# Fused attention and gMLP on one core: f32 loads cast on chip, half-size products paired in column halves, and a gMLP that runs without its lag

## The chip, the cores and the metric

The kernel runs on one core of one Trainium2 chip. The metric is device time in microseconds (us), the median of several runs. Engines are named as in the profile: PE is TensorE (matrix products), PEld its weight loads, DVE VectorE, ACT ScalarE, POOL GpSimd, SP SyncE (which here only issues transfers). In the traces below each engine takes its own instructions in the order of the program (VectorE's turns at 98.82 us, for example, behind five normalizations that they don't need), and the engines meet one another through semaphores. SBUF is the memory in which the kernel's tiles lie, PSUM the one in which this program puts PE's products. "Granted clock" is the share of full speed that PE was allowed.

## The reference, cut to what matters

There are 8 batches of 8 heads, 576 tokens, 64 numbers per head. Attention is causal with a window of 64 tokens; its result, 576 x 512 per batch, goes into a gated MLP that mixes over tokens.

```python
scores = scale * q @ k.T ; keep only 0 <= row - col < 64 ; attn = softmax(scores) @ v
x = attn.transpose(0, 2, 1, 3).reshape(8, 576, 512)
h = relu(x @ w_in)                         # w_in 512 x 1024
u, v = h[..., :512], h[..., 512:]
v_n = (v - mean(v)) / sqrt(var(v) + 1e-6)  # over the 512 features
v_s = w_spatial @ v_n + b_spatial          # over the 576 tokens
out = (u * v_s) @ w_out                    # w_out 512 x 512
```

## The kernel before

All inputs are f32 in DRAM; the products run in f16. The parts of the work have one-letter names that the whole text uses. For attention: T turns Q and K (VectorE transposes), S is the scores of two heads, E their exponential and mask, P the product with V and with ones. N1 and N2 are the logarithm and the exponential that turn P's row sums into reciprocals, and the multiplication that gives x. For the gMLP: V and U are the two halves of x @ w_in, L the normalization of V, G the product with w_spatial and the gate, O the product with w_out. W is the transposition of w_spatial, once.

V is needed at two alignments of 64 tokens, hence a copy shifted by 64 tokens ("vs" beside "vn").

```python
def load_qk(b, x, g, hp):                      # the load casts f32 to f16 on its way
    s = SRC[x][b, 4 * hp + g, :, :].rearrange("(k i t) d -> i k (t d)", i=32, t=2)
    nc.gpsimd.dma_start(NAT[b, x][32 * g:32 * g + 32, hp, :, :, :]..., s)

def emit_O(b, j):                              # 5 of them per batch, the fifth for 64 tokens
    po = mm(f"po{b}_{j}")
    for r in range(4):
        nc.tensor.matmul(po[0:jn, :], lhs, w_out_sb[r][:, :], start=(r == 0), stop=(r == 3))
    nc.scalar.copy(ob[0:jn, :], po[0:jn, :])
    (nc.scalar if b < 2 else nc.sync).dma_start(out[...], ob[0:jn, :])

def att_step(i, s, todo, before, between):     # one of the five steps of attention
    run_units(todo, before)                    # gMLP work first ...
    emit_S(i, s) ; post += [emit_E]
    emit_P(pb, ps_) ; post += [emit_N1, emit_N2]   # P of the step before
    while post:
        post.pop(0)()
        run_units(todo, between)               # ... and gMLP work between

for i in range(2, B + 2):                      # the steady state
    a, o = i - 1, i - 2                        # attention of i, gMLP of i-1, O of i-2
    st[0] = O(o);  st[1] = V(a);  st[2] = L(a), U0, U1, U2;  st[3] = G0, U3, G1, U4;  st[4] = G2, G3, G4
    # Q and K of batch i+1 are turned one piece per step, behind the steps 1 to 4 of batch i
    ...
```

So three batches are in work at a time: O lags the rest of its gMLP by one batch, and the turns of a batch stand in the steps of the batch before it. (The loop is shortened here.)

The softmax here doesn't subtract the row's maximum and nothing guards it: scores larger than these inputs give would overflow.

## Time and profile before

The kernel took 261.0 us at first; beside the changed kernel it took 262.45 us (median of 4 runs, 259.44 to 263.96). The profiled run has a span of 262.4 us.

| stage, by the start of V's first product of a batch | before, us |
|---|---|
| first scores | 20.2 |
| V of batch 0 | 36.2 |
| V of batch 1 | 84.5 |
| from V of batch 1 to V of batch 7, six periods | 155.2 |
| last three periods | 24.2, 24.2, 23.6 |
| the rest after V of batch 7 starts | 22.7 |

The page's busy line and its 40 slices, before. A digit is the busy share of a slice in tenths (a slice is 6.6 us), PEclk is the granted clock and DMA the mean busy share of the 16 DMA engines.

```profile
PE 218.9 (83%) x2899; PEld 111.8 (43%) x2899; DVE 154.8 (59%) x301; ACT 152.0 (58%) x283; POOL 151.5 (58%) x234
PE   8009884973965987998998699999999999999993
PEclk9756998696895799999999989999999999999999
DMA  8992499999999942995969995499330032004005
```

PE has holes in its first 23 slices, to about 151 us, and is full after that. There are two regimes, then: start-up and data at first, PE later. The DMA queues, before (packets, MB, share of 16 engines' span):

```profile
q0 software_dynamic: 46016, 12.27, 48.2%
q1 hardware_dynamic: 36816, 15.34, 25.6%
```

The view of windows for two late periods, before. Columns: window, its length, then busy time (and number) of PE, PEld, DVE, ACT, POOL, the granted clock, the DMA share and GB/s.

```profile
164.00:188.20 24.20, 23.89 (x359) 12.51 (x362) 17.70 (x35) 17.68 (x34) 17.60 (x27) 1.00 0.93 148
188.20:212.40 24.20, 24.10 (x359) 12.43 (x362) 17.72 (x35) 18.05 (x34) 5.82 (x7) 1.00 0.15 51
```

PE is busy 23.9 and 24.1 of 24.2 us: a late period is PE's work and almost nothing else. The view of waits, before: who waited for what, total us, times, longest us. These are PE's two largest.

```profile
PE sc L209 <- DVE tq L79: 14.2, 2, 13.6
PE oz L272 <- DVE x L300: 11.1, 12, 2.2
```

The first, all but 0.6 us of it, is the start (the first scores). No wait for x is longer than 2.2 us.

### The profile page before, as it was taken

How to read it: one execution, taken by the hardware profiler on the slowest of the kernel's cores; microseconds unless marked ns; L12 is line 12 of the kernel's file. 1: busy time of each engine (PE TensorE's matmuls, PEld its weight loads, DVE VectorE, ACT ScalarE, POOL GpSimd, SP SyncE). 2: the span in 40 equal slices, each digit the busy share in tenths (PEclk: the TensorE clock that was granted, in tenths of full speed). 3: DMA queues.
4: the chain of work that ended last, by engine and by line, in shares of the span. 5: the costliest groups of instructions: out<-in, count | busy, mean ns of one | idle time of the engine just before them, and what ended most of it. 6: DMA issues, size and time to landing. Idle time of an engine off the chain costs nothing.

```text
span 262.4 us, 6988 instructions
## 1 busy us (share of the span) xinstructions
PE 218.9 (83%) x2899; PEld 111.8 (43%) x2899; DVE 154.8 (59%) x301; ACT 152.0 (58%) x283; POOL 151.5 (58%) x234
## 2 busy tenths in 40 slices
PE   8009884973965987998998699999999999999993
PEld 2004541441534434544554345545544554554351
DVE  0076644353347598739770968397759757771740
ACT  2004962651276574576763685778687587856523
POOL 8631886599999979999863975985660000000000
PEclk9756998696895799999999989999999999999999
DMA  8992499999999942995969995499330032004005
GB/s 131 185 187 39 61 169 208 132 131 184 111 238 201 140 43 24 142 202 52 128 69 185 190 140 58 162 194 174 84 116 1 2 121 66 0 2 165 17 0 180
DMA packets 84175, 30.41 MB, mean 116 GB/s; under 512 B 77424, under 2 KB 79536, under 8 KB 84144
## 3 DMA queue, kind: packets, MB, share of 16 engines
q0 software_dynamic: 46016, 12.27, 48.2%
q1 hardware_dynamic: 36816, 15.34, 25.6%
q10 hardware_dynamic: 1312, 2.36, 2.7%
q8 instruction: 22, 0.36, 0.6%
q14 instruction: 9, 0.07, 0.1%
HBM read 32.79 MB, written 9.44 MB: 161 GB/s over the span
## 4 chain that ended last, share of the span: by engine, by line
PE 37%; DMA 17%; DVE 14%; POOL 14%; ACT 13%; issue 4%; ACTq 0%; DVEq 0%; POOLq 0%
PE ps L373 10%; PE po L394 8%; DMA out_dram<-ob 6%; DVE st L326 5%; PE pv L321 5%; DMA nq<-in_q_dram 5%; POOL nq L68 4%; POOL vs L122 3%; PE sc L209 3%; DVE x L300 3%; DMA nk<-in_k_dram 3%; PE oz L272 3%; POOL nk L68 3%; DMA wnat<-in_moe_w_spatial_dram 3%; ACT vs L324 2%
## 5 line engine op out<-in xcount | busy, mean ns | idle before, releaser
L122 POOL COPY vs<-vn 64x1024 f16<-64x1024 f16 (+1 forms) x44 | 42.5, 965 | 17.9 <-ACT vn L128 10.2
L249 ACT ACTIVATE e<-sc 128x1024 f16<-128x1024 f32 x32 | 32.7, 1021 | 21.5 <-PE sc L209 19.8
L68 POOL DMA_DIRECT2D nq<-in_q_dram x64 | 38.4, 616 | 10.0 <-issue 3.1
L373 PE MATMUL ps<-wspT,vn 128*128 128x512 f16 (+1 forms) x160 | 41.6, 393 | 2.8 <-DVE vn L343 2.6
L300 DVE TENSOR_TENSOR x<-oz,zi 128x512 f16<-128x512 f32 (+1 forms) x40 | 25.4, 634 | 30.3 <-ACT zi L298 26.4
L68 POOL DMA_DIRECT2D nk<-in_k_dram x64 | 38.6, 614 | 4.1 <-DMA wnat<-in_moe_w_spatial_dram 1.3
L321 PE MATMUL pv<-win,x 128*128 128x512 f16 (+1 forms) x160 | 39.6, 394 | 0.0
L394 PE MATMUL po<-wout,g 128*128 128x512 f16 (+1 forms) x160 | 38.0, 380 | 0.0
L209 PE MATMUL sc<-tq,tk 32*64 32x128 f16 (+2 forms) x1152 | 24.9, 222 | 15.1 <-DVE tq L79 14.2
L326 DVE BATCH_NORM_STATS2 st<-vs 128x6 f32<-128x512 f16 (+1 forms) x40 | 27.3, 683 | 14.4 <-ACT vs L324 14.1
L258 DVE TENSOR_TENSOR e<-e,mask 128x1024 f16<-128x1024 f16 x32 | 26.3, 822 | 15.4 <-ACT e L249 15.1
L397 ACT COPY ob<-po 128x512 f32<-128x512 f32 (+1 forms) x40 | 23.3, 583 | 20.7 <-PE po L394 12.8
L209 PEld LDWEIGHTS <-tk 32*64 32x64 f16 x1280 | 20.8, 109 | 32.1 <-issue 16.8
L353 PE MATMUL pu<-x,win 128*128 128x512 f16 x128 | 34.0, 406 | 0.0
L290 ACT ACTIVATE ln<-oz 128x512 f32<-128x512 f32 (+1 forms) x40 | 22.4, 560 | 10.4 <-PE oz L282 9.5
L324 ACT ACTIVATE vs<-pv 128x512 f16<-128x512 f32 (+1 forms) x40 | 23.5, 597 | 8.1 <-PE pv L321 7.3
L376 DVE TENSOR_TENSOR g<-ps,ru 128x512 f16<-128x512 f32 x32 | 21.1, 674 | 10.4 <-PE ps L373 10.2
L298 ACT ACTIVATE zi<-ln 128x512 f32<-128x512 f32 (+1 forms) x40 | 23.7, 592 | 1.3 <-ACT ob L397 0.8
L373 PEld LDWEIGHTS <-vn 128*128 128x128 f16 (+1 forms) x160 | 14.9, 100 | 22.4 <-DVE vn L343 7.1
L355 ACT ACTIVATE ru<-pu 128x512 f32<-128x512 f32 x32 | 18.9, 597 | 8.2 <-PE pu L353 8.1
L321 PEld LDWEIGHTS <-x 128*128 128x128 f16 (+1 forms) x160 | 14.6, 102 | 20.7 <-issue 6.7
L272 PE MATMUL oz<-e,onesK 128*64 128x512 f16 x64 | 13.2, 404 | 11.7 <-DVE x L300 9.4
(57 smaller groups left out, 256.4 us busy)
## 6 DMA issues: line engine op xcount, KB each, us to landing
vf<-in_v_dram SPq DMA_DIRECT2D x24, 256.0 KB, 5.5
out_dram<-ob SPq DMA_DIRECT2D x24, 256.0 KB, 2.1
nk<-in_k_dram POOLq DMA_DIRECT2D x64, 72.0 KB, 4.0
nq<-in_q_dram POOLq DMA_DIRECT2D x64, 72.0 KB, 4.2
out_dram<-ob ACTq DMA_DIRECT2D x8, 256.0 KB, 4.0
vf<-in_v_dram SPq DMA_DIRECT2D x15, 128.0 KB, 5.8
win<-in_moe_w_in_dram POOLq DMA_DIRECT2D x8, 128.0 KB, 5.1
out_dram<-ob SPq DMA_DIRECT2D x6, 128.0 KB, 2.3
```

Of the source, the lines that this page charges most:

```text
L68: nc.gpsimd.dma_start(NAT[b, x][32 * g:32 * g + 32, hp, :, :, :].rearrange("p k t d -> p k (t d)"), s)
L122: nc.gpsimd.tensor_copy(o, i)
L209: return [lambda e=e: nc.tensor.matmul(out, TR[b, "k"][rows, hp, 64 * key:64 * key + 64, e], TR[b, "q"][rows, hp, q0:q1, e], start=(e == 0 ...
L249: nc.scalar.activation(e2[:, :, :], sc[0][:, :, :], AF.Exp, bias=0.0, scale=0.125)
L258: nc.vector.tensor_tensor(e2[:, :, :], e2[:, :, :], m, ALU.min)
L300: nc.vector.tensor_tensor(x[:, 0:n], oz[:, 0, 0:n], zinv[:, 0:n], ALU.mult)
L321: nc.tensor.matmul(pv[0:jn, :], xcol(b, r, j), w_in_sb[r][:, 512:1024], start=(r == 0), stop=(r == 3))
L324: nc.scalar.activation(vs[0:jn, :], pv[0:jn, :], AF.Relu)
L326: nc.vector.bn_stats(st6[0:jn, 0:6], vs[0:jn, :])
L353: nc.tensor.matmul(pu[:, :], w_in_sb[r][:, 128 * m:128 * m + 128], X[b, r][:, :], start=(r == 0), stop=(r == 3))
L373: nc.tensor.matmul(ps[:, :], VN[b, kk][0:kn, 128 * m:128 * m + 128], wspT[kk][0:kn, 0:512], start=(kk == 0), stop=(kk == 4))
L394: nc.tensor.matmul(po[0:jn, :], lhs, w_out_sb[r][:, :], start=(r == 0), stop=(r == 3))
```

## The change

Its intent has four parts. (1) Q and K come as f32 through the hardware queues, in batch order, and are cast on chip. (2) POOL no longer issues 16 casting loads per batch, and from batch 3 on the shifted copy of V is made by a transfer instead of by POOL. (3) The 64-token remainders of V(b) and O(b-1) are computed as a pair, each in one half of PE's columns. (4) O is no longer a batch late: gMLP of batch a runs to its end, and the steps of attention of a+1 are set into it. The diff, cut to its core:

```diff
     def load_qk(b, x, h):
-        nc.gpsimd.dma_start(NAT[b, x][...], s)
+        nc.sync.dma_start(NF[b, x][...], s)              # f32
+    def cast_qk(b, x, hp, copy, p0=0, p1=128):
+        copy(NH[b, x][p0:p1, hp, :, :, :], NF[b, x][p0:p1, hp, :, :, :])
+    def shift_all(b):
+        nc.gpsimd.dma_start(vs[0:64, :, :, :], vn[0:64, :, :, :])
+        nc.gpsimd.dma_start(vs[64:128, 1:5, :, :], vn[64:128, 0:4, :, :])
 ...
+    def emit_VO4(b):                                      # "Q" in the sequences below
+        for r in range(4):
+            nc.tensor.matmul(pv[0:64, :], xcol(b, r, 4), w_in_sb[:, r, 512:1024], ...)
+            nc.tensor.matmul(pv[64:128, :], G[o, 4][:, 64 * r:64 * r + 64], w_out_sb[:, r, :], ...)
 ...
+    def att(i, s):
+        for f in state["post"]: f()
+        post = []
+        emit_S(i, s); emit_E(i, s)
+        emit_P(pb, ps_)
+        post += [lambda: emit_N1(pb, ps_), lambda: emit_N2(pb, ps_)]
+        state["post"] = post          # one is taken out after each following gMLP unit
 ...
+    def batch_in(b):
+        for hp in (0, 1):
+            for x in "kq":
+                cast_qk(b, x, hp, pool_copy)
+        for c in range(5):
+            cast_v_chunk(b, c, pool_copy)
+        if b < 3: (shifted copy by POOL)
+        else: shift_all(b)
+    for a in range(1, B):
+        load_batch(a + 2)
+        if a == 1: run(a, "p0034 o0 p0134 o1 p0234 o2 p0334 o3")    # V of batch 1
+        else:      run(a, "T0 V0 V1 V2 A0 V3" if a > 2 else "V0 V1 V2 V3")
+        if a > 2:  run(a, "Q A1 L U0 T1 U1 U2 U3 A2 U4 G0 G1 A3 G2 G3 G4 A4 O0 O1 O2 A5 O3")
+        else:      run(a, "Q L T0 U0 U1 A0 U2 U3 U4 A1 G0 T1 G1 G2 A2 G3 G4 A3 O0 O1 A4 O2 O3 A5")
+        batch_in(a + 2)
```

"T0" and "T1" turn the two halves of the heads of batch a+1, "A0" to "A5" are steps of its attention; the other letters are as above. The start is rewritten too: batch 0 is taken in two heads at a time, and POOL issues the weights' loads between its copies of V of batch 0 (w_in before the second step, the others before the fourth).

## The prediction

> **What bounds the kernel now.** From about 164 us on PE is the limit: in the windows view's stretches 164.0-188.2 and 188.2-212.4 us PE is busy 23.9 and 24.1 of 24.2 us at clock 1.00, DVE 17.7, ACT 18. A batch (gMLP of one, attention of another) costs 24.2 us of PE work. Before that, data is the limit. The timeline shows no scores until 20.2 us: the first turn waits for masks on DVE, they for POOL, which first issues 16 casting loads (0.6 us each, until 13.2 us). V of batch 0 starts at 36.2 us, the w_spatial transposes end at 48, and K and Q of batch 1 queue behind the weights (issued 40-54 us), so V of batch 1 starts at 84.5 us, V of batch 7 at 239.7: six batches at 25.9 us each. The tail is 22.7 us. The DMA table gives the software queue 48% of 16 engines' span: Q/K packets take 43-48 ns, the 256-byte V packets of the hardware queue 26 ns (first 30 us).
>
> **What changes.**
> 1. Q and K leave POOL's queue. The Trainium skill ("DMA: Bandwidth & Descriptors", SWDGE vs HWDGE vs iDMA) says only the software path casts during a transfer, hence the f32 buffers and on-chip casts. I estimate 512-byte hardware-queue packets at 30-35 ns (between V's 26 and the 2 KB stores' 82), so a batch needs about 17 us of the DMA engines, plus 3.4 us of stores: under the batch period.
> 2. POOL loses about 10 us a batch of issuing and, from batch 3, 5.5 us of shift copies (now DMAs); it gains four casts of 128x1152, about 1.4 us each by the 0.65 us of 128x512. It stays under 12 us a batch, off the chain. DVE gets its masks by 4 us.
> 3. V(b,4) and O(b-1,4) run in column halves. In the trace two 128*64 matmuls of the ones step take 0.24 us together, one 128*128 0.23. The skill ("TensorEngine Tiling (Array Packing)", Key Properties) calls such tiles independent; the trace agrees. Four matmuls hidden: 0.9 us, seven times, about 6 us, all on PE's chain.
> 4. O no longer lags; attention of a+1 fills gMLP of a: the same PE work.
>
> **Estimate.** Batch 0, consumed as it comes: first scores at 7-9 us, V(0) at 25. Batch 1 and 4.4 MB of weights need 29 us of DMA more: in by 46-48; W ends near 38, attention of 1 near 53. V(1) starts at 55 us (before 84.5): -29. Six periods of 23.3 us ideal, with 7 us of waits (mostly batch 2): 147 instead of 155: -8. Tail 22.7. Sum 225 us, range 214 to 240. Chances: faster 0.95, same 0.04, slower 0.01.
>
> **What would show it.** First scores before 10 us; V(1) at 50-60 us; late batches 23-24 us apart with PE over 95% busy; the last stretch as before; the hardware queues with over half of the DMA time, the software queue below 10%.
>
> **What would make it wrong.** 512-byte packets over 43 ns: then loads and stores fill the period and PE waits for casts. POOL casts over 2 us each beside DVE, so that turns at the head of DVE's queue block it. Weights landing after 45 us because three rings share the engines. Pairs that don't overlap: late periods stay at 24.2 us. A lower granted clock.

## The result, and the profile after

The change made the kernel slower: 298.1 us (median of 4 runs, 296.49 to 305.62), against 262.45 before. The ratio is 1.1435, with a 95% interval of 1.1315 to 1.1555. A ratio here, and in all experiments, is the mean time of one kernel's fast runs over that of the other's of the same rounds, so it is not quite the ratio of the medians quoted beside it. Executions over 1.5% slower than the fastest of the same kernel are left out of the means.

| stage | before | predicted | after |
|---|---|---|---|
| first scores | 20.2 | 7 to 9 | 13.0 |
| V of batch 0 | 36.2 | 25 | 40.0 |
| V of batch 1 | 84.5 | 55 | 86.4 |
| six periods | 155.2 | 147 | 188.4 |
| last three periods | 24.2, 24.2, 23.6 | 23 to 24 | 28.0, 26.5, 28.0 |
| rest | 22.7 | 22.7 | 21.8 |

The same lines of the page and of its queues, after (a slice is 7.4 us):

```profile
PE 219.7 (74%) x2893; PEld 116.9 (39%) x2893; DVE 162.0 (55%) x316; ACT 153.1 (52%) x279; POOL 86.4 (29%) x120
PE   7270789845667497395973979797989788797994
PEclk9685599985559689979899799997999999989999
DMA  9999999225784940787927789689969957002104
...
q1 hardware_dynamic: 75072, 33.04, 56.4%
q0 software_dynamic: 3024, 5.19, 9.2%
```

PE's busy time is the same as before (219.7 against 218.9 us), so nothing was added to PE; it has holes now, over the whole span, also where the DMA row says 0. POOL is down to 29%, as planned. Two late periods of the windows view, after (columns as before):

```profile
192.30:220.30 28.00, 24.43 (x356) 13.47 (x355) 17.86 (x35) 17.97 (x34) 8.86 (x11) 0.94 0.90 185
247.00:275.00 28.00, 24.43 (x355) 13.39 (x354) 15.80 (x32) 17.62 (x34) 0.00 (x0) 0.94 0.21 71
```

This pair answers the first suspicion, that f32 loads fill the DMA engines. In the first window they are 90% busy, in the last 21%, when all inputs have landed and POOL has nothing to do: both take 28.0 us. No other engine is over 18 us either. So neither bandwidth nor an engine's total is the limit of a late period. In both windows the granted clock is 0.94; the period between them (220.3 to 246.8 us) had 1.00, and there PE was busy only 22.9 of 26.5 us. So of the 28.0 us about 1.5 are PE's same work at the lower clock, and 3.6 are waiting. The view of waits, after, says what PE waits for:

```profile
PE oz L284 <- DVE x L312: 34.8, 21, 10.4
PE sc L221 <- DVE tq L101: 34.3, 11, 6.5
```

They were 11.1 and 14.2 us. The chain of waits, after, shows how one of the second kind arises; columns are start, length, what:

```profile
94.73 0.58 DVE st L345
95.33 0.18 DVE mv L346
95.54 0.31 ACT lnv L384
95.87 0.22 ACT rs L385
96.11 2.71 DVE vn L393 x5
98.82 0.69 DVE tk L101
99.51 0.67 DVE tq L101
100.22 1.07 PE sc L221 x26
```

The turns (tk, tq) of batch 2 need nothing of batch 1. But in VectorE's order they stand behind the five normalizations of batch 1 (vn), which wait for the statistics of all of V. PE stood still meanwhile, from 94.3 to 100.2. The other kind is in the same chain a little later:

```profile
116.63 0.59 ACT ob L445
117.25 0.34 ACTq L355
...
118.13 0.59 ACT ob L445
118.74 0.34 ACTq L355
...
119.12 0.64 ACT zi L310
119.78 0.70 DVE x L312
120.53 0.41 PE oz L284 x2
```

The next P (oz) waits for x of the step before it, since both use one PSUM tile. x waits for the exponential (zi), and the exponential stands behind output copies (ob) and the issue of their stores on ScalarE: the change emits N1 and N2 one at a time, each after a gMLP unit. Before, the same rule stood in the text, but the units between were V, U and G (short ScalarE work), and O stood in the first step only. Now O stands in the last steps, where attention of the next batch needs its last x at once.

**Theory A**, then: the order of work on the in-order engines ScalarE and VectorE (postponed N1 and N2, turns behind the normalization) makes PE wait, and this is what the late periods lost. **Rival B**: the f32 loads take too much of the DMA engines, or the weights take the place of batch 0. **Rival C**, for the middle (periods of 40.3 and 37.1 us): transfers wait for one another.

For C there was a sign in the view of waits of SP's queue, after; no such line exists before:

```profile
SPq L71 <- DMA out_dram<-ob: 41.8, 7, 11.8
SPq L84 <- DMA out_dram<-ob: 36.1, 5, 15.2
```

SP, at its loads of Q and K (L71) and V (L84), waits for stores of the output. No data passes between them. The compiled program shows why: all transfers of the hardware queues, loads and stores, take eight completion semaphores in turn, and each waits for the one eight before it. Part of SP's instruction list of the changed kernel, not of a profile:

```
16 L71 DMACopy fq_78<-in_q_dram 32x9x128 [waits DMAHW0_49]
17 L71 DMACopy fk_110<-in_k_dram 32x9x128 [waits DMAHW1_49]
18 L71 DMACopy fq_113<-in_q_dram 32x9x128 [waits DMAHW2_49]
...
44 L355 DMACopy out_dram<-ob_0_901 128x512 [waits DMAHW2_49,Activation_49]
```

The kept trace agrees: the transfers of SP and ScalarE carry eight semaphore numbers between them, POOL's eight others; a store that landed at 126.72 us, for example, and the load of V that was issued at 126.74 carry the same number. A load whose turn falls on a store's semaphore can't be issued before that store has been computed and written. That is this program's allocation of semaphores, not a fact of the chip. Before the change, Q and K used the software queue, which has eight of its own, so stores and most loads didn't share.

### The profile page after: what moved, and what is told of

Same layout as the page of the kernel before. It is cut to its first block, busy times and chain, and to the rows that moved or that the text cites. A ratio compares the mean times of both kernels' runs of the same rounds, so it can differ in the third digit from the quotient of the medians.

```text
span 296.6 us, 7014 instructions
## 1 busy us (share of the span) xinstructions
PE 219.7 (74%) x2893; PEld 116.9 (39%) x2893; DVE 162.0 (55%) x316; ACT 153.1 (52%) x279; POOL 86.4 (29%) x120
## 3 DMA queue, kind: packets, MB, share of 16 engines
q1 hardware_dynamic: 75072, 33.04, 56.4%
## 4 chain that ended last, share of the span: by engine, by line
PE 47%; DVE 21%; ACT 13%; DMA 11%; issue 4%; ACTq 2%; SPq 1%; DVEq 0%
PE ps L423 11%; PE pv L336 8%; DMA fq<-in_q_dram 6%; PE po L442 6%; PE sc L221 5%; DVE x L312 5%; DVE vn L393 5%; PE oz L284 4%; PE pu L403 3%; ACT e L261 3%; ACT zi L310 3%; PE oz L294 3%; ACT ob L445 2%; DVE e L270 2%; DVE tq L101 2%
## 5 line engine op out<-in xcount | busy, mean ns | idle before, releaser
L221 PE MATMUL sc<-tq,tk 32*64 32x128 f16 (+2 forms) x1152 | 26.9, 233 | 35.1 <-DVE tq L101 34.3
L270 DVE TENSOR_TENSOR e<-e,mask 128x1024 f16<-128x1024 f16 x32 | 25.1, 783 | 36.3 <-ACT e L261 36.1
L221 PEld LDWEIGHTS <-tk 32*64 32x64 f16 x1280 | 22.9, 115 | 50.8 <-DVE tq L101 24.1
L127 POOL CAST nk<-fk 128x1152 f16<-128x1152 f32 x12 | 14.2, 1180 | 89.1 <-DVE tk L101 60.6
L423 PE MATMUL ps<-wspT,vn 128*128 128x512 f16 (+1 forms) x160 | 38.0, 387 | 0.0
L127 POOL CAST vn<-vf 128x512 f16<-128x512 f32 (+1 forms) x40 | 25.1, 636 | 41.5 <-DMA vf<-in_v_dram 41.2
L336 PE MATMUL pv<-win,x 128*128 128x512 f16 (+1 forms) x132 | 34.8, 414 | 0.0
L445 ACT COPY ob<-po 128x512 f32<-128x512 f32 x32 | 18.8, 587 | 29.4 <-PE po L442 24.2
L442 PE MATMUL po<-wout,g 128*128 128x512 f16 x128 | 32.9, 404 | 0.0
L343 ACT ACTIVATE vs<-pv 128x512 f16<-128x512 f32 (+1 forms) x40 | 22.7, 599 | 12.8 <-PE pv L336 10.2
L426 DVE TENSOR_TENSOR g<-ps,ru 128x512 f16<-128x512 f32 x32 | 21.8, 683 | 10.2 <-PE ps L423 10.1
L127 POOL CAST nq<-fq 128x1152 f16<-128x1152 f32 (+1 forms) x16 | 19.7, 1231 | 23.5 <-DVE x L312 14.3
L310 ACT ACTIVATE zi<-ln 128x512 f32<-128x512 f32 (+1 forms) x40 | 23.6, 589 | 2.7 <-ACT ob L445 2.1
L284 PEld LDWEIGHTS <-onesK 128*64 128x64 f16 x80 | 6.9, 110 | 39.3 <-issue 37.8
L423 PEld LDWEIGHTS <-vn 128*128 128x128 f16 (+1 forms) x160 | 14.8, 99 | 16.8 <-issue 1.3
```

The source lines that it names most:

```text
L127: nc.gpsimd.tensor_copy(o, i)
L221: return [lambda e=e: nc.tensor.matmul(out, TR[b, "k"][rows, hp, 64 * key:64 * key + 64, e], TR[b, "q"][rows, hp, q0:q1, e], start=(e == 0 ...
L270: nc.vector.tensor_tensor(e2[:, :, :], e2[:, :, :], m, ALU.min)
L284: nc.tensor.matmul(oz[64 * h:64 * h + 64, 1, 0:n], onesK[:, :], e2[:, h, 0:n], start=True, stop=True)
L310: nc.scalar.activation(zinv[:, 0:n], lnz[:, 0:n], AF.Exp, bias=0.0, scale=-1.0)
L336: nc.tensor.matmul(PV[b, j][0:jn, :], xcol(b, r, j), w_in_sb[:, r, 512:1024], start=(r == 0), stop=(r == 3))
```

## The experiments

Fifteen kernels were built on the changed kernel (or on the kernel before, where said), and three small ones measured costs by themselves. The kernel before was timed in each group: 263.68, 263.74, 262.86, 262.51 and 261.92 us, and once, 263.23 us, beside e18. In the second group (e5 to e8) only two of its seven runs count as fast, in the third (e9 to e12) three of eleven, so ratios there hang on few runs.

### e1: N1 and N2 at once

```diff
-            post += [lambda: emit_N1(pb, ps_), lambda: emit_N2(pb, ps_)]
+            emit_N1(pb, ps_)
+            emit_N2(pb, ps_)
```

> The changed kernel with one edit: the two normalizing steps of an attention step (Ln, then Exp and the multiply) are emitted at once, before the copies of the units that follow, and not one after each unit. Theory (order in the in-order queues): in each batch the ones matmul waits for x before attention steps A4 and A5 (0.5 and 1.2 us in the last full period, 2.8 and 3.1 us in the period that starts at 126 us) because Ln and Exp stand behind output copies on ACT; these waits should shrink below 0.5 us, late periods fall from about 28 to 26-27 us, the two slow periods by 4-6 us each, the total from 297 to about 280. Rival (DMA bound: Q/K packets slower than estimated, 90 to 96% DMA busy in late periods): the total stays within 2% of 297.

Measured: 286.46 us, ratio to before 1.0833 (1.0745 to 1.092; fast runs 283.7 to 286.6). The profiled run was an odd one of 665.79 us, with PE 98% busy and clock 1.000; I have no explanation and read nothing from it.

### e2: turns ahead of the normalization

```diff
-            run(a, "T0 V0 V1 V2 A0 V3" if a > 2 else "V0 V1 V2 V3")
-            run(a, "Q A1 L U0 T1 U1 U2 U3 A2 ...")
-            run(a, "Q L T0 U0 U1 A0 U2 U3 U4 A1 G0 T1 G1 ...")
+            run(a, "T0 T1 V0 V1 V2 A0 V3" if a > 2 else "V0 V1 V2 V3")
+            run(a, "Q A1 L U0 U1 U2 U3 A2 ...")
+            run(a, "T0 T1 Q L U0 U1 A0 U2 U3 U4 A1 G0 G1 ...")
```

> The changed kernel with one edit: both transposes of the next batch stand at the start of the batch (before LN), not behind the five LN subtractions on DVE. Theory: PE's wait for tq (5.9 us at 94-100 us, 3.6 at 135-138, 1.9 in each late period) goes, and with it the slower PE clock after it (about 1.4 us in a late period): late periods from 28 to 24.5-25.5 us, total from 297 to about 275-280. POOL's casts of the next batch start earlier too, since their buffer comes free earlier. Rival (DMA bound): total within 2% of 297; second rival (transposes now wait for late casts at the head of DVE's queue): new DVE waits for POOL nk or nq, no gain.

Measured: 287.39 us, ratio 1.0876 (1.0785 to 1.0968). Late periods 25.4, 24.6, 25.9 us, where they were 28.0, 26.5, 28.0. PE's waits of e2:

```profile
PE oz L284 <- DVE x L312: 33.3, 21, 8.6
PE sc L221 <- DVE tq L101: 20.1, 6, 7.3
```

The edit takes 14 us off the waits for the turns and leaves the waits for x alone, as it should.

### e3: weights behind batch 0

The weights' loads are issued by POOL only after it has cast a K of batch 0's last heads, so they can't get ahead of batch 0.

```diff
-        if s == 1:
-            load_win(1); load_win(0)
...
-            pairs_in(0, s + 1, dve_copy, act_copy)
+            pairs_in(0, s + 1, pool_copy if s == 2 else dve_copy, act_copy)
+        if s == 2:
+            load_win(1); load_win(0)
```

> The changed kernel with one edit: the weight loads are issued behind a POOL cast of the last head pair of K of batch 0, so that they no longer share the DMA engines with batch 0. Theory (2 KB weight packets of about 95 ns alternate with 512-byte packets of about 40 ns, so that weights took 85% of the engines at 20-30 us and the last pair of batch 0 landed at 28.5 us): the last pair lands by 23 us, V of batch 0 starts at 30-33 us instead of 40. The engines are busy until 55 us either way, so V of batch 1 moves less, from 86 to 78-84 us; total 3 to 8 us less. Rival (only the sum of bytes counts): V of batch 1 and the total unchanged.

Measured: 296.89 us, but three of its four runs are slow (the profiled one 316.03 us at clock 0.702; its only fast run 290.49). Alone it is inconclusive. What the weights do to the start can still be read in the changed kernel's trace: from 20 to 30 us the software queue's 1426 packets took 84.9% of the DMA engines (95 ns each) and the 1423 of Q and K 34.4% (39 ns), and the chain has a load of Q that took 13.31 us, to 28.5 us.

### e4: all three

> The three edits together. Theory: they act at different places, so gains add: total about 255 to 265 us, late periods 23.5-24.5 us. Rival (DMA bound in late periods at 48 ns a Q/K packet: 25 us a period): late periods stay at 26 us or more as long as loads run and only the last full one gets shorter.

Measured: 278.06 us, ratio 1.0534 (1.0455 to 1.0612), above the range expected. V of batch 0 starts at 32.6 us (40.0 in the changed kernel), V of batch 1 at 75.2 (86.4). PE's three largest waits of e4:

```profile
PE sc L221 <- DVE tq L101: 21.2, 10, 7.0
PE oz L294 <- DMA vs<-vn: 14.5, 2, 7.3
PE oz L284 <- DVE x L312: 6.1, 8, 1.6
```

One of its late periods in the windows view, columns as before:

```profile
177.60:201.00 23.40, 22.96 (x356) 12.44 (x355) 17.86 (x34) 17.12 (x33) 7.15 (x9) 1.00 1.03 214
```

The wait for x is down from 34.8 to 6.1 us, and this period takes 23.4 us with the DMA engines busy throughout. The other two late ones took 24.5 and 26.4 us (28.0, 26.5 and 28.0 in the changed kernel); in the last the clock was 0.94 again, and PE waited 1.5 us for a turn. Theory A holds for the late periods, and the bandwidth part of rival B falls there: PE is full while the f32 loads stream. By the medians the three edits together gain 20 us, and e1 and e2 alone gained about 12 and 11; by the ratios it is 24, 16 and 15, since the changed kernel was timed in another group (ratio 1.1435).

The middle is another matter (31.7, 36.9 and 33.9 us, against 40.3, 37.1 and 28.5). Its chain, e4:

```profile
119.06 7.96 DMA vs<-vn
...
139.29 2.05 DMA out_dram<-ob
...
143.28 8.09 DMA vf<-in_v_dram
...
153.62 5.65 DMA vs<-vn
```

A shifted copy of V, sent as a transfer, took 8.0 and 5.7 us behind the other loads, and a load of V could be issued only once a store had landed (rival C). In the changed kernel itself nothing waits for the shifted copy (its view of waits has no such line; e4's has 14.5 us): this wait came to light only when the orders were mended.

### e5 and e6: longer rows, fewer loads

e5 (on e4) gives each partition 18 consecutive tokens, so a row of a load has 4,608 bytes instead of 512; VectorE's transposes then write with a stride. e6 adds to e5 one load for four heads instead of four.

```diff
-        s = SRC[x][b, h, :, :].rearrange("(k i t) d -> i k (t d)", i=32, t=2)
+        s = SRC[x][b, h, :, :].rearrange("(i j) d -> i (j d)", i=32)
...
-        nc.vector.transpose(o.rearrange("p (k i t) -> p k t i", i=32, t=2), ...)
+        nc.vector.transpose(o.rearrange("p (i j) -> p j i", i=32), ...)
```

> On the kernel with all three edits (278 us): each partition takes 18 consecutive tokens of a head, so that a Q or K load has rows of 4608 bytes in place of 9 rows of 512; the transposes put the tokens back in order. Same bytes, same number of loads, same waits in the program. Theory (a batch of loads costs 25 us of the DMA engines with 512-byte packets at 41 to 57 ns, and the weights and three batches queue up): Q/K packets vanish as a cost, DMA busy in late periods falls from 90% to 50-65%, the total falls by 8 to 18 us to 260-270. Rival (loads wait for the completion counter of an earlier store, not for bandwidth): the middle periods stay at 32-37 us and the total falls by less than 4 us.

> As the run with long rows, and for batches 2 to 7 one load for four heads of K or Q: 9 loads a batch in place of 21, the same packets. Theory of the shared completion counters (eight for all hardware DMAs of both queues, handed out in turn; a load waits for the DMA eight before it, which may be a store of a batch still being computed): SP's waits for stores (52 us in the kernel with all three edits) fall below 25 us and the total by 4 to 10 us against the run with long rows. Rival (bandwidth alone): no difference over 1%.

Measured: e5 282.84 us, ratio 1.0861; e6 278.03 us, ratio 1.0697. In e5 the packets of the hardware queue fell from 75,072 to 42,304, and the time did not fall. It was longer than e4's; a strided transpose took 1.24 us instead of about 0.75, which may be why. The middle periods (33.8, 37.3, 33.7 us, together 104.8) were no shorter than e4's (102.4), so longer rows as tried here gain nothing; what they would gain without the slower transposes was not measured. e6 had half of SP's waits for stores (34.3 us instead of 66.7), and its time is 4.8 us below e5's (its six periods are 7.7 us shorter together): fewer transfers mean fewer turns on shared semaphores. That supports rival C, but see e15.

### e7: the shifted copy by POOL again

```diff
-        if b < 3:
+        if True:
             for p in range(4):
                 shift_pair(b, p, pool_copy)
```

> On the kernel with all three edits (278 us): the shifted copy of V is made by POOL for every batch as for batch 2, and not by a DMA from SBUF to SBUF. Theory: the two waits of the weighted-sum matmuls for that DMA (14.5 us together; it landed 8.0 and 5.7 us after its issue, among the loads of the next batch) shrink, since POOL is 33% busy and a copy of a batch takes 5.2 us but the first pair of heads is ready after 1.3 us: total 267 to 273. Rival: the copies take POOL's time before the next casts, total unchanged within 1%.

Measured (on e4): 260.22 us, ratio 1.000 (0.9828 to 1.0173; the runs of the kernel before in this group scatter, and its median was 263.74). The six periods fell from 176.7 to 165.3 us (e7's profiled run, 263.54 us, is slow, so its periods are, if anything, too long), and instead of 14.5 us for the transfer PE waited once for POOL's copy:

```profile
PE oz L294 <- POOL vs L127: 4.9, 1, 4.9
```

By the medians this one edit gains 18 us, more than expected. A copy that POOL makes in about 0.6 us a piece, on an engine with time to spare, had been turned into a transfer whose latency stood on the chain. With this the change's loss is gone, but not more.

### e8: the sum of what seemed to help

> Long rows, fewer loads, shifts on POOL, and the order of the late batches for batch 2 as well, on top of the three edits. Theory: the middle periods fall to 24-27 us, late ones stay at 23.5-25, V of batch 1 at 68-73 us: total 238 to 252, faster than the kernel before (263). Rival: some other limit in the first 110 us keeps it above 258.

Longer rows, fewer loads, POOL's copy and the late order already from batch 2: 273.34 us, ratio 1.0512, far above the range expected. Its second and third period are short (26.6, 26.3 us), the first is not (35.8), and its late ones are 27.3, 27.6, 26.7 us. It has e5's strided transposes on VectorE, and e7 without them has 23.4 to 24.0. The reading that they are the cause fits e5 and e6 (25.1 to 27.2), and PE's longest waits in e8's late periods are for the mask step on VectorE (6.8 us in all, 1.9 in e7's), but it was not tried by itself.

### e9 and e10: the pairs alone

e9 is the kernel before with the pairs of V and O, and nothing else; e10 is e7 without them.

> The kernel before with one part of the change alone: V of 64 tokens and O of 64 tokens of the batch before in column halves. Theory (prediction, step 3): four matmuls a batch are hidden where PE is the limit; late periods 24.2 to 23.3-23.5 us, total 262 to 256-259 (2%). Rival (the evacuation of both halves stands in one more unit on ACT, or the alternation costs PE): late periods stay at 24.2 and the total within 1%.

> The kernel with three edits and V's shift on POOL (260 us), with the pairs taken apart: V of 64 tokens, then O of 64 tokens. Theory: its late periods, 23.4 to 24.0 us, grow by 0.9 us each, the total by 4 to 6 us. Rival: no change over 1%.

Measured: e9 258.53 us, ratio 0.9944 (0.9852 to 1.0037). e10 263.76 us, ratio 1.013 (1.0043 to 1.0216), that is 1.3% above e7, which was timed on another chip with its own runs of the kernel before; the two intervals overlap. In the trace a pair's two products do run at the same time (e4; each of these two takes half of PE's columns):

```profile
181.82 0.40 PE L370 MATMUL pv<-win,x 128*64 128x512 f16 x1
181.82 0.41 PE L372 MATMUL pv<-wout,g 128*64 128x512 f16 x1
```

The next pairs start 0.21 to 0.24 us apart, about as far as single products of full width (seven of them take 1.67 us just before). So the Trainium skill's statement that tiles run independently ("TensorEngine Tiling (Array Packing)", Key Properties) holds for this kernel. The gain is 1.5 us in e9, whose interval includes none (4.3 us by the medians of all runs), and about 3.4 us in e10, not certain either: below the 6 us predicted. A late period of e10 is 0.3 to 0.4 us longer than one of e7 (23.8, 24.5, 23.8 against 23.4, 24.0, 23.4), not 0.9. PE's work did fall as predicted: in these periods PE was busy 23.0 us in e7 and 23.8 to 23.9 in e10. But without the pairs PE has hardly a hole (23.75 of 23.75 us in the first), and with them it waits 0.4 to 1.1 us: half of what was saved was lost to waiting, for the mask step above all.

### e11 and e12: stores out of the loads' way

e11 (on e7) stores through POOL's software queue, which has other semaphores, and puts the casts of the next batch right after the pair. e12 gives batches 1 and 2 the late order too.

```diff
-        (nc.scalar if b < 3 else nc.sync).dma_start(out[...], ob[...])
+        nc.gpsimd.dma_start(out[...], ob[...])
...
-            run(a, "Q A1 L U0 ...")
+            run(a, "Q C A1 L U0 ...")          # C: batch_in(a + 2)
```

> The kernel with three edits and V's shift on POOL (260 us), with the stores on POOL's software queue, and the casts of the next batch placed before them in POOL's order. Loads then share their eight completion counters with loads alone. Theory: SP's waits for stores (51 us) vanish; the wait for V of batch 4 at 136-150 us, which runs from an output copy over its store to the issue of V's load, goes; the period from 136 us falls from 32.7 to 26-28 us, the total to 250-256. Rival (bandwidth: 45 us of DMA for two batches): the load is late all the same, total within 1% of 260.

> As the run with stores on POOL, and batches 1 and 2 in the order of the late batches: the transposes and two attention steps stand before LN. Theory: in the periods of batches 1 and 2 the chain runs on DVE alone for 10 us (statistics, transposes, LN, then the mask of the first attention step) and PE waits; with the step in front these periods fall from 30-32 us to 25-27, the total to 240-247, faster than before by over 5%. Rival (data of batch 2 and 3 is late and now stands at the head of DVE's queue): no gain, total at 250 or more.

Measured: e11 287.58 us (281.75 to 289.04; three of four runs are slow), e12 288.8 us, ratio 1.1086: both far slower than expected. SP's waits for stores between loads did vanish, and the last input had landed by about 170 us. But the late periods now took 30.4 to 31.2 us, except the last (23.4 us in both), in which POOL had nothing left to cast. The timeline of VectorE and POOL, e11 (start, length, engine, line, operation, output <- inputs):

```profile
177.04 1.16 POOL L127 CAST nk<-fk 128x1152 f16<-128x1152 f32 x1
177.49 7.85 DVE L270 TENSOR_TENSOR e<-e,mask 128x1024 f16<-128x1024 f16 x1
178.13 1.15 POOL L127 CAST nq<-fq 128x1152 f16<-128x1152 f32 x1
...
181.40 2.83 POOL L127 CAST vn<-vf 128x512 f16<-128x512 f32 x5
184.19 2.94 POOL L127 COPY vs<-vn 64x512 f16<-64x512 f16 x4
```

A mask step of VectorE, which takes 0.65 us alone (e14), lasted 7.85 us, from just after the start of POOL's first cast until past the end of its last. In e12 this happened five times (7.9 to 8.05 us), in e11 three times. In the changed kernel no mask step took over 1.51 us: the hold is no part of its loss. The Trainium skill ("SBUF — State Buffer", "SBUF: two separate sides") says that VectorE and POOL share a pair of ports as an exclusive lock, for the whole instruction, when VectorE has two inputs in SBUF and POOL's instruction reads SBUF; the mask step has, and the casts do. Here it lasted much longer than one instruction of POOL.

### e13: Q and K by casting loads again

On e7: Q and K of batches 2 to 7 come by the software queue straight into f16, which takes four large casts per batch from POOL and 16 loads per batch from the shared semaphores. Batches 1 and 2 have the late order. Two things come with it: the f16 tiles of Q and K have two buffers instead of one, and the loads of batch 2 are issued in another order.

```diff
-        nc.sync.dma_start(NF[b, x]...)
+        (nc.sync if b < 2 else nc.gpsimd).dma_start((NF if b < 2 else NH)[b, x]...)
...
-        for hp in (0, 1):
-            for x in "kq":
-                cast_qk(b, x, hp, pool_copy)
...
-            run(a, "T0 T1 V0 V1 V2 A0 V3" if a > 2 else "V0 V1 V2 V3")
+            run(a, "T0 T1 V0 V1 V2 A0 V3")     # and the order of a > 2 for all a
```

> Three edits and V's shift on POOL (260 us), with Q and K of batches 2 to 7 loaded by casting loads of the software queue as in the kernel before (no casts on POOL for them, 30 hardware DMAs fewer in the queue of eight counters), and batches 1 and 2 in the order of the late batches. Batches 0 and 1 keep the hardware loads. Theory: V of batch 1 stays near 74 us, the periods of batches 1 to 3 fall from 30-33 to 24-27 us, total 238 to 248, 6 to 9% faster than before. Rival (the middle periods are held by bandwidth or by the order alone): 252 us or more.

Measured: 249.97 us (248.7 to 251.84), ratio 0.9544 (0.9477 to 0.9612). It beats both kernels: the verdict on record is "unclear", but its six runs all lie below all eleven of the kernel before (260.47 and up). That is a little above the 238 to 248 expected. Two of its periods in the windows view:

```profile
156.00:179.50 23.50, 23.01 (x356) 12.49 (x355) 18.29 (x34) 18.44 (x35) 15.13 (x24) 1.00 0.60 111
179.50:202.90 23.40, 22.96 (x356) 12.45 (x355) 17.28 (x34) 17.90 (x35) 12.88 (x21) 1.00 0.75 145
```

A late period is 23.4 us with PE busy 23.0, about what the prediction called ideal (23.3), and all six together are 151.0 us. How much each of e13's edits gives was not separated.

### e14 to e18: costs by themselves, and the row of casts

e14, e16 and e18 give a wrong result. e14 loads two batches of K (16 loads) first by the hardware queue as f32, then the next two by the software queue with the cast, and runs VectorE's operations alone and beside POOL, each of whose operations waits for the one before it.

> Not the computation (its result is wrong on purpose): costs by themselves, one after the other. First 16 loads of K (512-byte rows, f32) on the hardware queue, then the same 16 with the cast on the software queue, then four loads of V; then the DVE operations of the kernel alone (four rounds) and beside ten casts and ten 64-partition copies on POOL. Theory 1: a 512-byte packet costs 40 ns or more on the hardware queue, no less than on the software queue (prediction: 30 to 35). Theory 2: the mask step (both inputs in SBUF) and the LN step wait while POOL works: several of them take over 1.5 us, the statistics, the transposes and the product that reads PSUM keep their time. Rival to 2: durations are the same as alone.

Measured, in one run: the hardware queue took from 0.74 to about 14.8 us, the software queue from 15.62 to 27.57. So with nothing else running the software queue was not slower, 12.0 us against 14.1; it wrote half the bytes and needed no cast afterwards. Beside POOL's casts the mask step rose from 0.65 to 1.39 to 1.48 us and the normalization from 0.40 to 0.62; statistics, products from PSUM and transposes did not change.

e15 breaks the row of casts in e12: after each cast POOL copies one column of it, so that POOL must wait for its own result.

```diff
+    def pool_cast(o, i):
+        nc.gpsimd.tensor_copy(o, i)
+        nc.gpsimd.tensor_copy(brk[0:n, :], <last column of o>)
```

> The kernel of e12 with one thing added: behind each of the nine casts of a batch POOL copies one column of what it has just cast, so that POOL has to wait for its own last result before it goes on. Theory (a train of POOL casts that wait for nothing keeps VectorE's mask step out until the train ends): the mask steps of 7.9 to 8.05 us fall under 2 us, the late periods of 30.8 to 31.2 us fall to 24 to 26, and the time falls from 288.8 to 250 to 262. Rival (the mask step is slowed in proportion to POOL's busy time, or the late periods come from something else that moving the stores brought, such as the place of the casts): POOL's busy time is the same or longer, the mask steps stay near 7.9 us or the periods stay near 30.8, and the time stays at 285 to 292.

Measured: 264.78 us, ratio 1.0088 (1.002 to 1.0155), where e12 had 1.1086. No mask step after 60 us took longer than 1.47 us. One of the longest, in the timeline of e15:

```profile
172.57 1.46 DVE L280 TENSOR_TENSOR e<-e,mask 128x1024 f16<-128x1024 f16 x1 [0.60 <-ACT e L271]
```

All 32 mask steps together take 26.5 us, against 58.3 in e12. So the unbroken row of casts was what slowed e12, and by about 24 us. The time came out a little above the range, and so did three middle periods (29.2, 29.2, 28.1). e15 also bears on rival C and on e13. No load of Q, K or V waits for a store in it, and all batches have the late order; yet its six periods take 166.1 us, e7's 165.3. Its stores now stand behind POOL's casts and copies (one had to wait until 161.0 us), so the trial isn't clean. But neither free loads nor the late order is shown to be worth anything by itself, and what made e13 faster is more likely in its casting loads and second buffers (not shown).

> The costs by themselves as in e14 (result wrong on purpose), but each of the ten POOL casts writes a tile of its own, so that no cast waits for the one before it. Theory: one mask step of VectorE beside this train takes 8 to 12 us (the rest of the ten casts), where it took 1.4 to 1.5 us in e14. Rival (the sharing is by the operation, whatever the casts wait for): all mask steps stay at 1.0 to 1.6 us.

> Four sections by themselves (result wrong on purpose): in each POOL runs the eight casts of a batch in a row, every one into a tile of its own, while VectorE runs two rounds of statistics, mask and product. Sections one and two: the casts wait for nothing; three and four: each cast also waits for the loads of its data, which have long landed. In sections two and four the first mask step also waits for an exponential of ScalarE, as in the kernel. Theory left after e16 (VectorE is held out for the whole row where the casts carry waits of their own, as in e12, and not where they carry none): the first mask step takes 1.0 to 1.6 us in sections one and two and 5 to 7 us in three and four. Rival (it is VectorE's own wait for ScalarE that lets POOL's row go first): 5 to 7 us in sections two and four. If all four stay at 1.0 to 1.6 us, the cause of the 7.9 us is in neither and stays open.

e16 repeats e14 with casts that wait for nothing, ten in a row; e18 adds casts that wait for landed loads, and mask steps that wait for ScalarE. Measured: mask steps of 1.26 to 1.30 us in e16. In e18 the first mask steps took 1.35 us (casts without waits, mask after ScalarE), 1.40 us (casts with waits, mask without) and 0.69 us (both); one of the planned sections missed its row, because POOL started later than planned, and e16 stands for it. No long hold appeared. What a row must have besides to hold VectorE out for 7.9 us stays open. That breaking the row ends it in the kernel is shown.

e17 is e13 with the same breaks behind V's casts.

> The kernel of e13 (Q and K of batches 2 to 7 cast by the loads, POOL left with V's casts and the shifted copies) with the same column copies behind the V casts. Theory: in e13 these casts wait for their V chunks one by one, so there is hardly a train to break; 249 to 251 us, within 1% of e13. Rival (the two engines still lose time to one another in e13): 246 us or less.

Measured: 248.83 us, ratio 0.945 (0.9366 to 0.9535); one of its four runs, the profiled one, is slow. The interval overlaps that of e13, so the break is not shown to help there; the periods are the same 23.4 us. e13 and e17 are the best versions found.

## Why the prediction was wrong, point by point

The prediction was 225 us, range 214 to 240; the kernel took 298.1. Span against sum: V of batch 1 is late by 31 us, the six periods are long by 41, the rest is short by 1.

- **"O no longer lags; attention of a+1 fills gMLP of a: the same PE work."** This step failed. PE's work was the same or less (24.4 us busy of 28.0 at clock 0.94, 22.9 of 26.5 at 1.00). But I costed it as a sum of busy time and left out what each step has to wait for. Without the lag, a product of PE follows soon after the ScalarE and VectorE work that it needs, and those two take their work in order. PE's waits for x and for the turns rose from 25 us to 69. e1 and e2 took off about 12 and 11 us, each undoing one of the two orders; with both (and the weights moved) the late periods were 23.4, 24.5 and 26.4 us. In the changed kernel these two make up 69 of the 73 us that PE waits in the view. Yet undoing them, with the weights' move, gained only 20 us: some waits for turns remained (21.2 us in e4), and another wait, hidden until then, came up behind them (the next point but one).
- **"Six periods of 23.3 us ideal, with 7 us of waits."** The ideal is right: e4 and e13 have 23.4. The 7 us were mis-sized: 188.4 us were measured, 48 over six ideal ones. On the way to e13 they came off in three parts: 11.7 us by the orders and weights (e4: 176.7), 11.4 by the shifted copy (e7: 165.3), 14.3 by e13's edits together (151.0). That leaves about 10.6.
- **"From batch 3, 5.5 us of shift copies (now DMAs)."** I counted them as relief of POOL, which had time to spare, and gave the transfer's latency no place. It took 5.7 and 8.0 us on the chain (e4), and undoing it was worth about 5%, 18 us by the medians (e7). In the changed kernel PE was still held elsewhere and nothing waited for it.
- **Loads that wait for stores** are not in the prediction. They come from shared completion semaphores, and I had not read the program's list of waits for it. What they cost stays open: e6 with half of these waits was 4.8 us faster than e5, e15 without them no faster than e7.
- **"V(0) at 25" and "V(1) starts at 55."** Measured 40.0 and 86.4. The weights share the engines with batch 0 (a load of Q took 13.3 us), which the prediction put among the dangers but not in the sum. After V(0) no transfer is on the chain at all until V(1): W's last transposition waited for a copy on VectorE behind the normalization (to 52.8 us), and then each step of attention of batch 1 waited for its cast and turn. I had assumed that data was all that bound this part. V(0) to V(1) takes 41 to 46 us in every version from e4 on that has the new order (46.3 in the changed kernel, 48.2 before), so the orders tried here don't cure it; what would is open.
- **"512-byte hardware-queue packets at 30-35 ns."** Too low: 41.6 ns in the first 10 us (1396 packets, 36.3% of 16 engines) and 45 ns alone in e14 (4780 packets, 112.9% of 16 engines in 12 us; the views count overlapping packets, hence over 100%). But it is not the cause in the late periods: the last one, with 21% DMA, was as slow; and e5 with long rows gained nothing, though its transposes were slower. The danger that I named first came true and cost little.
- **Pairs, "about 6 us".** The mechanism is right and so is PE's saving (0.8 us a period against 0.9); but only 0.3 to 0.4 us of it became time in e10 against e7. The totals, 1.5 us in e9 and 3.4 in e10, are both not certain.
- **What held.** First scores came earlier (13.0, not 7 to 9, against 20.2), POOL fell from 151.5 to 86.4 us busy, the software queue to 9.2%, POOL's casts of 128x1152 took 1.18 us, and the rest after V(7) stayed as it was. None of this was where the time was lost. The granted clock fell too (0.885 against 0.922 in the profiled runs): in the after kernel 0.94 in the late periods of 28.0 us and 1.00 in the one of 26.5, though all three have holes. At 0.94 the same PE work takes about 1.5 us more. The prediction had named a lower clock among its dangers; what lowers it isn't shown here.

That moving Q and K to the hardware queues would pay was my inference; the section of the skill that the prediction cites only says which path can cast. e14 shows no gain in the loads themselves, and e13, which takes the path back for six batches, is faster (with other edits beside it).

## What to carry to other kernels

A schedule that takes a lag out must be costed as a chain, not as a sum: write down for each product which ScalarE and VectorE instruction it needs, and what stands before that one in the engine's own order. Put short work that others wait for (a reciprocal, a turn) ahead of long work that nobody waits for yet. Before moving work from an idle engine to a transfer, ask what the transfer's latency is under load, and whether its completion semaphore is shared with something that is computed much later; and where VectorE's masks run beside a row of POOL's casts, look at the length of single instructions, since sums don't show a hold.

## What the Trainium skill lacked or had wrong

- "SBUF — State Buffer" (SBUF: two separate sides) says that the second of a VectorE and a POOL instruction blocks for the whole of the first. In e11 and e12 a mask step was held for 7.85 to 8.05 us, through nine POOL casts in a row, and a one-column copy between the casts ended it (1.46 us in e15). The page doesn't say that a hold can span several instructions. In e14, e16 and e18 it spanned one (0.65 us became 1.07 to 1.52), so when it does is open.
- "DMA: Bandwidth & Descriptors" (Issuing engine by pattern) calls the hardware queues generally faster. For 16 loads of K with 512-byte rows of f32, e14 shows, in one run, 14.1 us by the hardware queue and 12.0 us by the software queue with the cast to f16.
- The same page (Why a DMA increments its semaphore by 16 and not by 1) asks for a semaphore per slot in flight. It doesn't warn that slots which loads and stores share make a load wait for a store: 41.8 and 36.1 us of waits on SP in the changed kernel.
- The same page (Specifications) gives 512 bytes as the least transfer for line rate. In e14, loads with 512-byte rows moved 193 GB/s with the DMA engines full (2 to 14 us), and the stores at its end, with 2,048-byte rows, 345 GB/s (84 to 110 us). One is a load into 32 partitions each and the other a store from up to 128, so this is no clean pair, but 512-byte rows were far from the rate that these engines reached.
